# A fused attention and SiLU kernel: first keys by another queue in fp32, wider first products, a last product in two halves

## The chip, the cores and the metric

The kernel runs on one core of a Trainium2 chip. The metric is the device time of one execution in microseconds, the median of three runs. The profile is of one further execution; its span runs from the first to the last instruction.

## The reference

```python
def _attn_ref(q, k, v):                       # (8, 12, 448, 64) each
    scale = 1.0 / np.sqrt(q.shape[-1])
    scores = scale * np.matmul(q, k.transpose(0, 1, 3, 2))
    ...
    attn = attn / (np.sum(attn, axis=-1, keepdims=True) + 1e-09)
    return np.matmul(attn, v).astype(np.float32)

def _moe_ref(x, w_in, w_out):                 # (3584, 768), (768, 2048), (2048, 768)
    h = x @ w_in
    g = h * (1.0 / (1.0 + np.exp(-h)))
    return (g @ w_out).astype(np.float32)
```

The attention's output, with tokens ahead of heads, is `x`. Inputs and output are fp32.

## The kernel before

**Work units.** A unit is one batch and a group of four heads: 8 x 3 = 24 units. A unit's keys and queries are each one tile of 128 partitions (four heads of 32) by 14 x 64 elements: partition i of a head holds tokens 14i to 14i + 13. POOL loads them with a DMA that casts fp32 to fp16 (`load_k` L314, `load_q` L319). Queries of the first unit come in two halves of seven tokens (`PIECES` L253). VectorE then turns blocks of 32 x 32 pairs (`turn_k` L375: per key tile two transposes of six blocks, L387, and one "lone" of two, L390; `turn_q` L392), so that TensorE has head elements on partitions.

**Attention.** Scores are computed with keys on the partitions and queries along the columns (`score` L436, four heads at a time in strips of 32 rows). A unit's 14 blocks of 32 keys go in chunks of four; the fourth chunk is half a unit and is shared with the next unit. ScalarE takes exponentials of 896 elements from three PSUM tiles in turn (`expo` L479). Sums and products with V are matmuls of 32 columns of weights (`attend_alone` L535 and L558, L591); VectorE inverts the sums and normalizes into `xT`, scaled by one half (`norm` L642). The first unit's first two bursts of scores use half of the queries each, so burst (0, 0) needs all key chunks but the lone one, and only the first half of q.

**First products.** `ffn1` (L684) multiplies blocks of 128 columns of `w_in` (f = 0 to 15) with `xT`, six matmuls for the six parts of 128 of the model dimension. All matmuls of this and the next stage are issued by `times` (L670, so L673 in the profile). ScalarE takes a tanh (`tanh` L702), VectorE multiplies it into the gate (`gate` L734, L740 for batch 0): (1 + tanh(h/2)) h/2 is the SiLU. In batch 0 the tokens come in two pieces of 224; two blocks f and f + 1 share one PSUM bank of 448 columns (`blocks` L699 is 2 for batch 0, 1 elsewhere), so every matmul there has 224 columns. Batches 1 to 3 use 448 columns. Batches 4 to 7 go in pairs with seven products in place of eight (`pair_product` L833).

**Last products.** Output rows go in quads of two tiles of 128 tokens (14 quads). The first quad is computed plainly (`plain` L926, o in the profile). The others split the weights and the gates into halves and use seven products m = 1, 5, 6, 2, 7, 3, 4 of eight matmuls of 384 columns (`product` L910; p in the profile). Products 1, 6, 7 and 4 gather in one PSUM bank, 5 and 3 in a second, 2 in a third. `take_copy` (L976) copies products 1, 5, 6 and 4 to SBUF on ScalarE, `take_sum` (L981) adds 2, 7 and 3 to such copies on VectorE, and `store` (L956) sends a 128 x 384 part to HBM by SP's queue, in the last quads by SP's and ScalarE's queues in turn. Of the last quad, product 4 comes last: eight matmuls, ScalarE's copy, two stores of 64 rows.

**The order.** Nothing is left to a scheduler at run time. The class `Order` (L111) plays the engines' times through while the kernel is built: each `Op` has an engine, a duration that the author estimates, and dependences, and the loop at L1880 picks what each engine does next, lowest bias first; the order so found is the program's order on each engine. Loads go out on POOL in the order of L1039 to L1066 (`od.load`, L155), at most eight at once; a key tile's buffer is one of two (`NRK` L242), so the third keys wait for the first to be turned. Where the planner expects TensorE to wait in the early stage it fills with matmuls of zeros (`run_zeros` L1867); the first fill is `FIRST` = 47 blocks of 128 columns (L248) in matmuls of up to 512. The zeros' tile is VectorE's first memset (L285).

Of the kernel before, what the change touches and what calls it, by code (L numbers as in the profile page):

```python
# [9 lines left out]
FP16 = mybir.dt.float16  # L10
# [100 lines left out]
class Order:  # L111
# [48 lines left out]
    def step(self):  # L160
# [26 lines left out]
        elif self.pool:  # L187
# [9 lines left out]
            if at is not None and at <= self.now:  # L197
# [6 lines left out]
                few = len(self.sent) < 7  # L204
# [10 lines left out]
def kernel(  # L215
# [27 lines left out]
    PACE = 2.6  # L243
    NPL = 4
# [3 lines left out]
    COLD, FIRST, QUIET = 8.5, 47, 0.16  # L248
    SHY = 0.5
    AWAIT = 1.0  # L250
    FAR = (NT * B // 4 - 3, NT * B // 4 - 1)
# [66 lines left out]

    def load_q(n, g0, g1):  # L319
# [55 lines left out]
    def turn_k(b, hg):  # L375
        t = rawk[(b, hg)][:].bitcast(FP32).rearrange("p (g i) -> p g i", i=32)
        kt = sb.tile([128, TPP, 32, 2], FP16, name=f"KT_{b}_{hg}", tag="KT", bufs=3)
        KT[(b, hg)] = kt
        pairs = kt.rearrange("p g i e -> p (g i e)").bitcast(FP32)
# [3 lines left out]
        for x in (0, 2):  # L383
# [3 lines left out]
            nc.vector.transpose(out=full[:, x : x + 2], in_=toks[:, :, at : at + 3])  # L387
            if count == 4:
                lone = 12 * (not high)
                nc.vector.transpose(out=pairs[:, lone : lone + 2], in_=toks[:, :, 3 - 3 * at])  # L390
# [293 lines left out]
    def ffn1(b, f, t0, t1, strips, c0, c1):  # L684
        i = f % blocks(b)
# [13 lines left out]
    def blocks(b):  # L699
        return 2 if b == 0 else 1  # L700

    def tanh(b, f, t0, t1):  # L702
        n = (t1 - t0) * blocks(b)
# [30 lines left out]
    def gate(b, f, t0, t1):  # L734
        r = b % 2
        cut = 6 * 128 - S if b == 1 else S
        for lo, hi, dst, at in ((0, cut, G, S * r), (cut, S, X, -cut)):
            lo, hi = max(lo, t0), min(hi, t1)
            if b == 0 and lo < hi:
# [170 lines left out]
    def product(qd, m, f0, f1, strips):  # L910
        w = {1: rows(2 * qd, 0), 2: rows(2 * qd, 1), 4: rows(2 * qd + 1, 1), 7: rows(2 * qd + 1, 0)}
        w = w[m] if m in w else S_t[(qd, m)]
        if BANK[m] == m and f0 == 0:
            pr_t[(qd, m)] = psum_bank(f"p_{qd}_{m}")
        for f in range(f0, f1):
            times(
                pr_t[(qd, BANK[m])][:, 0:OH],
                w[:, f, :],
                W_[m][:, f, :],
# [60 lines left out]

    def take_sum(qd, m):  # L981
# [57 lines left out]
    plan_k(0, 0)  # L1039
# [36 lines left out]

    def plan_turn(n):
        b, hg, g0, g1 = units[n]
        if b == B - 1 and not rq_ring.can(1, od.now):
            return False  # L1080
        if (b, hg) not in kt_op:
            if not kt_ring.can(1, od.now):
# [4 lines left out]
                    "DVE", 0.73, lambda: turn_k(b, hg), [ld_k[(b, hg)]], 20, then=rk_ring.give  # L1087
                )
            )
        if b == B - 1:  # L1090
# [7 lines left out]
                    [load],  # L1098
                    20,
# [38 lines left out]
    def gates_at(t, f):  # L1138
# [3 lines left out]
        for b in {(128 * t + c) // S for c in (0, 127)}:  # L1142
            x = g_op.get((b, f), [])
            made += x if len(x) >= (len(PIECES) if b == 0 else 1) else [None]
        return made

    def queue_ffn1(b, g0, g1):
        t0, t1, parts = 32 * g0, 32 * g1, []
        begun = {}
        for f in range(NFF) if b == 0 else [x for f in range(HF if b < PB else FILL) for x in (f, f + HF)]:  # L1150

          half = 6 if b else NDC
          for c0 in range(0, NDC, half):

            def run(f=f, c0=c0):
# [5 lines left out]
                n = blocks(b)  # L1161
# [27 lines left out]
            def deps(f=f, c0=c0):  # L1189
                if c0:  # L1190
                    return [] if begun.get(f) == c0 else [None]
                if f % blocks(b) and f - 1 not in parts:
                    return [None]
                made = [(x_op[(b, cc, g0)], cc * mm(t1 - t0)) for cc in range(NDC)] + ld_win[f]
# [11 lines left out]
            moe.append((deps, int(f % blocks(b) == 0 and c0 == 0), run, ()))  # L1206
# [762 lines left out]
```

## Time and profile before

| | |
|---|---|
| median of 3 runs | 380.81 us (380.5 to 380.94) |
| profiled execution | 380.37 us |
| its span | 378.6 us |
| TensorE busy | 372.4 us |
| ScalarE, VectorE busy | 255.5, 269.7 us |
| DMA bytes counted on the queues | 34.47 MB |
| q0 (POOL's loads) | 22.82 MB, 40.3% of 16 engines' span |
| q1 (SP's stores) | 10.53 MB, 10.6% |
| granted TensorE clock | 1.000 |

The page counts an engine busy from an instruction's start to its end. Matmuls overlap, so a busy TensorE says only that one was in flight; how fast they follow each other is read from their starts. The timeline lists instructions in order of time, merged when equal ones follow each other: start, busy time, engine, line, operation, tiles, shapes and count, and in brackets the idle time before them with what ended it. The chain of waits follows the end back to the start. The q0 rows of the DMA packets show the bytes written, so a packet of 1792 bytes in fp16 has read twice as many.

### The profile page before, as it was taken

To read this page: it belongs to the slowest core of one execution; us is meant where nothing else is said; L and a number is where in the kernel's file an instruction comes from. 1 tells how busy PE (TensorE), PEld (TensorE's weight loads), DVE (VectorE), ACT (ScalarE), POOL (GpSimd) and SP (SyncE) were. 2 spreads that over 40 slices of the span, in tenths; PEclk is the share of its full clock that TensorE was granted. 3 is DMA by queue.
4 is the path that set the end of the run, shared out by engine and by line. 5 is a ranking of instruction groups with operands and counts; after the bars stand their busy time and mean duration, and the time that the engine had idled before them with its cause. 6 is when DMAs were issued, how large, how long until landed. Compare 5 with 4: busy or idle time off the path is not lost.

```text
span 378.6 us, 9949 instructions
## 1 busy us (share of the span) xinstructions
PE 372.4 (98%) x4024; PEld 191.5 (51%) x4024; DVE 269.7 (71%) x553; ACT 255.5 (67%) x400; POOL 84.9 (22%) x155
## 2 busy tenths in 40 slices
PE   7999999999999999999999999999999999999995
PEld 3367664444444444444444454545555555556663
DVE  3666859899995869995969998898475424446541
ACT  4988874897768787877788777658872238882221
POOL 6652438451007326006423200000000000000000
PEclk9999999999999999999999999999999999999999
DMA  7999999946139948148955421200002331002343
GB/s 120 191 208 210 206 204 186 190 53 98 17 92 124 184 49 124 26 94 116 170 86 73 54 53 34 68 18 0 3 1 59 94 74 26 0 2 59 84 110 83
DMA packets 35854, 34.47 MB, mean 91 GB/s; under 512 B 11872, under 2 KB 35040, under 8 KB 35808
## 3 DMA queue, kind: packets, MB, share of 16 engines
q0 software_dynamic: 25312, 22.82, 40.3%
q1 hardware_dynamic: 10080, 10.53, 10.6%
q8 instruction: 31, 0.51, 0.5%
q10 hardware_dynamic: 416, 0.49, 0.4%
q14 instruction: 15, 0.12, 0.1%
HBM read 45.61 MB, written 11.01 MB: 150 GB/s over the span
## 4 chain that ended last, share of the span: by engine, by line
PE 97%; DMA 1%; ACT 1%; DVE 0%; issue 0%; POOLq 0%
PE p L673 32%; PE h L673 21%; PE f L673 16%; PE s L438 12%; PE a L558 8%; PE o L673 3%; PE a L544 2%; PE a L591 2%; DMA rk<-in_k_dram 1%; ACT T L483 1%; PE z L1872 0%; PE z L673 0%; PE z L544 0%; DVE KT L387 0%; ACT ost L977 0%
## 5 line engine op out<-in xcount | busy, mean ns | idle before, releaser
L494 ACT ACTIVATE E<-s 128x896 f16<-128x896 f32 x164 | 142.0, 923 | 23.7 <-PE s L438 23.6
L673 PEld LDWEIGHTS <-w_in_t 128*128 128x128 f16 (+1 forms) x981 | 61.3, 97 | 45.2 <-issue 8.4
L673 PE MATMUL h<-xT,w_in_t 128*32 128x448 f16 (+2 forms) x834 | 84.0, 333 | 0.0
L344 POOL DMA_DIRECT2D V<-in_v_dram x88 | 48.4, 557 | 52.5 <-PE a L558 32.2
L673 PEld LDWEIGHTS <-G 128*128 128x128 f16 (+1 forms) x637 | 43.4, 97 | 32.4 <-issue 5.2
L977 ACT COPY ost<-p 128x384 f32<-128x384 f32 x52 | 24.9, 479 | 50.4 <-PE p L673 31.9
L705 ACT ACTIVATE th<-h 128x448 f16<-128x448 f32 x67 | 36.6, 546 | 22.8 <-PE h L673 19.1
L673 PE MATMUL p<-w_out_t,G 128*128 128x384 f16 (+1 forms) x343 | 51.9, 326 | 0.0
L438 PE MATMUL s<-rq,KT 32*128 32x448 f16 (+3 forms) x728 | 45.4, 347 | 1.3 <-DVE rq L402 1.0
L983 DVE TENSOR_TENSOR ost<-p,ost 128x384 f32<-128x384 f32 x39 | 21.6, 553 | 31.3 <-PE p L673 14.3
L673 PEld LDWEIGHTS <-S 128*128 128x128 f16 (+1 forms) x330 | 29.5, 98 | 23.5 <-issue 4.2
L673 PE MATMUL p<-D,S 128*128 128x384 f16 (+1 forms) x214 | 37.5, 326 | 0.0
L558 PE MATMUL a<-E,V 128*32 128x448 f16 (+1 forms) x640 | 32.9, 356 | 0.0
L749 DVE SCALAR_TENSOR_TENSOR G<-th,h 128x448 f16<-128x448 f16 (+1 forms) x52 | 28.8, 565 | 4.5 <-ACT th L705 3.9
L324 POOL DMA_DIRECT2D rq<-in_q_dram x25 | 13.8, 553 | 67.3 <-PE s L438 57.7
L661 DVE SCALAR_TENSOR_TENSOR xT<-a,rdn 128x448 f16<-128x448 f32 x46 | 27.0, 618 | 2.7 <-PE a L558 2.0
L438 PEld LDWEIGHTS <-KT 32*128 32x128 f16 (+1 forms) x824 | 12.5, 96 | 30.3 <-issue 28.1
L507 DVE TENSOR_TENSOR T<-T,E 128x1792 f16<-128x1792 f16 x20 | 21.7, 1086 | 3.9 <-ACT E L494 3.8
L876 DVE TENSOR_TENSOR p<-f,p 128x448 f32<-128x448 f32 x15 | 9.4, 624 | 20.4 <-PE f L673 13.5
L673 PE MATMUL f<-sx,tw 128*128 128x448 f16 x102 | 23.5, 352 | 0.0
L507 DVE TENSOR_TENSOR T<-E,E 128x1792 f16<-128x1792 f16 x20 | 21.6, 1082 | 2.5 <-ACT E L494 2.5
L558 PEld LDWEIGHTS <-V 128*32 128x32 f16 (+1 forms) x640 | 13.7, 95 | 18.0 <-issue 10.3
(95 smaller groups left out, 430.2 us busy)
## 6 DMA issues: line engine op xcount, KB each, us to landing
out_dram<-ost SPq DMA_DIRECT2D x194, 48.0 KB, 1.6
rk<-in_k_dram POOLq DMA_DIRECT2D x24, 224.0 KB, 5.0
rq<-in_q_dram POOLq DMA_DIRECT2D x23, 224.0 KB, 5.6
w_out_t<-in_moe_w_out_dram POOLq DMA_DIRECT2D x4, 768.0 KB, 12.5
V<-in_v_dram POOLq DMA_DIRECT2D x42, 64.0 KB, 4.1
V<-in_v_dram POOLq DMA_DIRECT2D x42, 48.0 KB, 4.3
w_in_t<-in_moe_w_in_dram POOLq DMA_DIRECT2D x6, 256.0 KB, 9.0
w_in_t<-in_moe_w_in_dram POOLq DMA_DIRECT2D x3, 512.0 KB, 12.3
```

What stands on the lines that cost most here:

```text
L324: nc.gpsimd.dma_start(out=rawq[n][:, cols], in_=group_of(q, b, hg)[:, cols])
L344: nc.gpsimd.dma_start(out=VT[b][32 * x : 32 * (x + 1), hs, at : at + count, :], in_=v[b, hs].rearrange("h (i g) d -> i h g d", g=TPP)[:, : ...
L438: nc.tensor.matmul(out=pS[p0 : p0 + 32 * (x1 - x0), h % 2, at : at + q1 - q0], lhsT=KT[(b, hg)][32 * h : 32 * (h + 1), key_rows(b, hg, c, ...
L494: nc.scalar.activation(out=E[(n, w)][:, 2 * y : 2 * y + 2, :], in_=pS_t[(n, w, y)][:, :, 0:S], func=AF.Exp, scale=attn_scale,)
L507: nc.vector.tensor_tensor(out=T[n], in0=T[n] if step else E[(n, 0)], in1=E[(n, step + 1)], op=ALU.add,)
L558: nc.tensor.matmul(out=a[32 * h : 32 * (h + 1), 0:S], lhsT=VT[b][k0:k1, HG * hg + h, place(b, hg, c), part - 1 :: 2], rhs=e[k0:k1, h], sta ...
L661: nc.vector.scalar_tensor_tensor(out=x3(b, cc)[:, cc % 3, 32 * g0 : 32 * g1], in0=acc[(n, part)][:, 0:nq], scalar=0.5, in1=rdn_t[n].rearra ...
L673: nc.tensor.matmul(out=out[i : i + cut], lhsT=w[:, i : i + cut], rhs=x, start=start, stop=stop, skip_group_check=True,)
L705: nc.scalar.activation(out=th, in_=h_t[(b, f, t0)][:, 0:n], func=AF.Tanh)
L749: nc.vector.scalar_tensor_tensor(out=dst[:, f, at + lo : at + hi], in0=th_t[(b, f, t0)][:, lo - t0 : hi - t0], scalar=1.0, in1=h_t[(b, f, ...
L977: nc.scalar.copy(out=ost(qd, *OUT[m]), in_=bank(qd, BANK[m]))
L983: nc.vector.tensor_tensor(out=t, in0=bank(qd, BANK[m]), in1=t, op=ALU.add)
```

## The change

**The first keys.** `rk_0_0` isn't loaded by POOL any more. SP issues two loads in fp32 to a scratch tile (in the tenth buffer of the exponentials): tokens 0 to 7 of each row (128 x 512 elements) and 8 to 13 (128 x 384). ScalarE casts each piece to fp16. VectorE's turning of the first keys is split: first six blocks, q's first half, the other six blocks, the lone two, q's second half. POOL's first load is then q's first half, and all later loads move up by one place. The first fill of zeros is 36 blocks of 128 columns. Turning of the first four units gets an earlier bias, which moves a few transposes ahead of normalizations.

**First products of batch 0.** Blocks 0 to 5 stay as they were. Blocks 6 to 15 are queued once both pieces are there, as ten blocks of 448 columns with one PSUM bank, one tanh and one gate each. There were 192 matmuls of 224 columns; there are 72, and 60 of 448.

**The last product.** In the last quad, product 2 is computed in two halves of 192 output columns, each with a PSUM bank of its own, sixteen matmuls of 192 columns. Three of them stand ahead of product 3's first half, three ahead of product 4, two behind it, and the eight of the second half end the program. VectorE adds each half to the copy of product 1; the first half is stored by SP (128 x 192), the second by SP and ScalarE (64 x 192 each). Product 3 is cut in two around product 7. Otherwise the order of TensorE's instructions is the same, but for the zeros: behind the first scores there are 1152, 1024, 1280 and 1792 columns of them in place of 1408, 1152, 1024 and 1664, and one more matmul of 256 columns stands ahead of the first products with V.

```diff
+    BF0 = 6
...
-    COLD, FIRST, QUIET = 8.5, 47, 0.16
+    COLD, FIRST, QUIET = 8.5, 36, 0.16
+    FIRST_K = ((0, 8, 3.45), (8, TPP, 4.3))
...
+    def load_first():
+        t = sb.tile([128, HG, S], FP16, name="first_k", tag=f"E{NE - 1}", bufs=1)
+        t = t.rearrange("p h s -> p (h s)").bitcast(FP32)
+        rawk[(0, 0)] = sb.tile([128, TPP * D], FP16, name="rk_0_0", tag="rk", bufs=NRK)
+        for g0, g1, _ in FIRST_K:
+            first_k[g0] = t[:, D * g0 : D * g1]
+            nc.sync.dma_start(out=first_k[g0], in_=group_of(k, 0, 0)[:, D * g0 : D * g1])
+
+    def cast_first(g0, g1):
+        nc.scalar.copy(out=rawk[(0, 0)][:, D * g0 : D * g1], in_=first_k[g0])
...
-    def turn_k(b, hg):
+    def turn_k(b, hg, parts=(0, 2, 3)):
...
+            if x in parts:
+                nc.vector.transpose(out=full[:, x : x + 2], in_=toks[:, :, at : at + 3])
...
+        if 3 in parts:
+            nc.vector.transpose(out=lone[0], in_=lone[1])
...
-    def blocks(b):
-        return 2 if b == 0 else 1
+    def blocks(b, f):
+        return 2 if b == 0 and f < BF0 else 1
...
-    def product(qd, m, f0, f1, strips):
+    def product(qd, m, f0, f1, strips, c0=0, c1=OH):
...
+            pr_t[(qd, m)] = psum_bank(f"p_{qd}_{m}" + "r" * (c0 > 0))
...
-                pr_t[(qd, BANK[m])][:, 0:OH],
+                pr_t[(qd, BANK[m])][:, 0 : c1 - c0],
                 w[:, f, :],
-                W_[m][:, f, :],
+                W_[m][:, f, c0:c1],
...
+    def take_end(p, c0, c1):
+        t = ost_t[(LAST, 0, 0)][:, c0:c1]
+        nc.vector.tensor_tensor(out=t, in0=p, in1=t, op=ALU.add)
+        row = out.shape[0] - 256
+        for lo, eng in ((0, nc.sync), (64, nc.scalar)) if c0 else ((0, nc.sync),):
+            hi = lo + 64 if c0 else 128
+            eng.dma_start(out=out[row + lo : row + hi, c0:c1], in_=t[lo:hi])
...
-    plan_k(0, 0)
+    od.emit(load_first)
+    rk_ring.take()
+    cast_op = []
+    for g0, g1, at in FIRST_K:
+        come = Op("SP", 0.0, None)
+        come.done = at
+        fn = lambda g0=g0, g1=g1: cast_first(g0, g1)
+        cast_op.append(od.add(Op("ACT", act(D * (g1 - g0)), fn, [come], -10)))
...
+    def turn_bias(n):
+        return -11 if n <= 3 else 20
...
+            for part, busy, x in ((0, 0.37, 0), (2, 0.33, 1), (3, 0.2, 1)):
...
-        for f in range(NFF) if b == 0 else [x for f in range(HF if b < PB else FILL) for x in (f, f + HF)]:
+        for f in range(BF0 * (g1 - g0 == TPP), NFF if g1 - g0 == TPP else BF0) if b == 0 else [x for f in range(HF if b < PB else FILL) for x in (f, f + HF)]:
...
-        for m in (1, 5, 6, 2, 7, 3, 4):
+        for m in (1, 5, 6, 2, 7, 3, 4) if qd < LAST else (1, 5, 6, 7, 3, 4):
             for f0 in range(0, HF, 1):
                 queue(m, f0, f0 + 1)
+        if qd == LAST:
+            for c in range(2):
+                for f0 in range(0, HF, 1):
+                    queue(2, f0, f0 + 1, OH // 2 * c, OH // 2 * (c + 1))
...
+        if b == 0 and not pieces_left[b]:
+            queue_ffn1(b, 0, TPP)
```

The two numbers in `FIRST_K` are the times, in the planner's own clock, at which it takes the two pieces to have come.

## The prediction

> **What bounds the kernel now.** I read the page first, then the chain of waits, then the timeline of the first 75 us and of the last 6, then the DMA packets and landings in the trace. The page:
>
> ```profile
> span 378.6 us, 9949 instructions
> ## 1 busy us (share of the span) xinstructions
> PE 372.4 (98%) x4024; PEld 191.5 (51%) x4024; DVE 269.7 (71%) x553; ACT 255.5 (67%) x400; POOL 84.9 (22%) x155
> ```
>
> TensorE is busy for all but 6.2 us. So only three things can shorten the kernel: what TensorE waits for at the start, columns that it need not stream, and what stands behind its last product. The start, in the chain of waits:
>
> ```profile
> 1.25 3.77 DMA rk<-in_k_dram
> 5.02 0.02 issue
> 5.04 0.38 DVE KT L387
> 5.42 0.12 DVE KT L390
> 5.55 0.26 DVE KT L387
> 5.81 0.30 DVE rq L402
> 6.11 0.04 issue
> 6.15 0.63 PE s L438 x16
> 6.78 2.52 ACT T L483 x3
> ```
>
> The first keys take 3.77 us from POOL's issue to their landing, then four transposes, then the first scores at 6.15. The timeline beside it:
>
> ```profile
> 1.00 4.13 PE L1872 MATMUL z<-zeros 128*128 128x512 f16 x12 [1.00 <-DVE zeros L285]
> ...
> 1.25 0.68 POOL L316 DMA_DIRECT2D rk<-in_k_dram  x1 [0.80 <-POOLq L1953]
> ...
> 1.93 1.09 POOL L324 DMA_DIRECT2D rq<-in_q_dram  x2
> ...
> 6.76 3.35 ACT L483 ACTIVATE T<-s 128x896 f16<-128x896 f32 x4 [4.74 <-PE s L438]
> ...
> 9.97 9.86 ACT L494 ACTIVATE E<-s 128x896 f16<-128x896 f32 x12
> ```
>
> ScalarE runs exponentials without a break from 6.76 to 19.83; until about 11 us TensorE waits for it and fills with zeros. From 11 us on the starts of the matmuls leave no gap but about 0.1 us at each change between row, column and full products. So a start that is earlier by x is worth x, if loads keep up. The 16 DMA engines have packets without a break from 2.64 us (the first) to beyond 56 us.
>
> **A, the first keys.** Removed: POOL's first issue (0.68), so q's first half is issued at 1.25 instead of 1.93. Added: two issues on SP, two casts on ScalarE. SP has nothing ahead of them, ScalarE is idle until 6.76 but for its table load (over at 2.0).
> - *First packet.* No load on SP's queue is in the trace. SP can issue from 0.74 (when ScalarE starts) to 1.25 (when POOL does). Stores on that queue show their first packet 1.13 us after the issue (375.24 to 376.36); POOL's load took 1.39. I take 0.74 + 1.13 = 1.87, 0.77 earlier than 2.64; the late end is 1.25 + 1.39, no gain. The Trainium skill ("DMA: Bandwidth & Descriptors", Specifications) gives first-byte latencies of about 0.6 us for the hardware queues and 1 us for POOL's; by its difference of 0.4 instead of my 0.26 the packet, and the sum below, would gain 0.14 more.
> - *Landing.* A 1792-byte cast packet takes 154 ns, a 1536-byte store packet 65, a 4-byte one 9: by 9 ns + bytes/27.4, 2048 bytes take 84 and 1536 take 65. Eight of each per engine: 0.67 and 0.52 us, 1.19 together, against 8 x 154 = 1.23 before. From first packet to full landing the old load took 5.02 - 2.64 = 2.38, 1.15 beyond its packets; the last store 0.57 beyond. q's first half (8 x 88 = 0.70) mixes with the second piece. The second piece lands between 1.87 + 1.19 + 0.57 = 3.63 and 1.87 + 1.19 + 0.70 + 1.15 = 4.91; I take 4.27. q's first half lands between 4.33 and 4.91.
> - *Casts.* No such row. Copies of 384 from PSUM take 0.48, exponentials of 896 take 0.92, by the line 0.49 and 0.60 for 384 and 512. The first (and the first transpose) lies under the second landing.
> - *First scores.* By the keys: landing + 0.03 + cast 0.49 + 0.03 + transpose 0.34 + 0.05 = 4.57 to 5.85. By q: landing + its transpose 0.37 + the second key transpose 0.32 + 0.05 = 5.07 to 5.65. So 5.07 to 5.85; I take 5.40, which is **0.75 earlier** (0.3 to 1.08). The lone transpose now stands behind the first scores.
> - *What is late next.* Fills behind the point where TensorE stops waiting for ScalarE grow from 1664 to 1792 columns and one of 256 is added ahead of the first products with V: 384 columns at 0.218 us per 512 are 0.16, and a change of mode 0.10. The third unit's q is transposed ahead of a normalization now, and a wait of 0.08 at 17.28 may go. Net 0.18: **A = 0.57** (0.1 to 0.9).
> - *Loads.* They stay saturated, so each lands earlier by as much as the first packet, 0.77, as the keys' packets cost the same. V landed at 14.62 for use at 14.71; the last quarter of w_out at 56.21 for the product at 56.39. So everything ahead of 56 us may gain 0.77 + 0.18 = 0.95 at most: A and B below need 0.71.
>
> **B, 448 columns wide.** 120 products of 224 columns become 60 of 448; tanh and gate operations stay 16 each, with the same elements.
>
> ```profile
> 32.99 2.47 PE L673 MATMUL h<-xT,w_in_t 128*128 128x224 f16 x24
> ...
> 56.39 1.47 PE L673 MATMUL o<-w_out_t,G 128*32 128x384 f16 x32
> ...
> 71.28 2.44 PE L673 MATMUL h<-xT,w_in_t 128*128 128x448 f16 x12
> ```
>
> From start to start, without the change of mode, the 24 take 96.1 ns each and the 12 take 189.9. 2 x 96.1 - 189.9 = 2.3 ns, 60 times: **B = 0.14**. The wide blocks need both halves of the tokens, which are made before the first of them stands in the order; blocks 8 to 15 come later than before, so w_in (last landing 35.70, first use 36.78) gets more room.
>
> **C, the end.**
>
> ```profile
> 373.23 1.46 PE L673 MATMUL p<-D,G 128*128 128x384 f16 x8
> 373.50 0.56 DVE L983 TENSOR_TENSOR ost<-p,ost 128x384 f32<-128x384 f32 x1 [0.74 <-PE p L673]
> 374.73 0.48 ACT L977 COPY ost<-p 128x384 f32<-128x384 f32 x1 [4.72 <-PE p L673]
> 375.24 0.50 ACTq L970 DMA_DIRECT2D out_dram<-ost  x1
> ```
>
> Call 374.69, where TensorE ends, X. Then came 0.04, the copy 0.48, 0.03, and two stores whose last landing is 377.62, 2.38 after their issue: X + 2.93. Now sixteen products of 192 take the place of eight of 384 (162.6 ns each). The spacing of 192 is not shown; between 82.5 (the warm 128-column fill at 7.01 is followed after 57 ns, so weights do not hold it) and 97 (a weight load's own time): 0.02 to 0.25 more, I take 0.02. Ten follow product 4, so its copy and both its stores are issued by X + 0.25. The first half's store follows on SP until X + 0.61. The second half is added by VectorE, 0.11 after X + 0.02 (as at 373.50), 0.36 long (0.56 for 384; L876's 448 take 0.62, so 1.03 ns an element), so ScalarE's store goes out at X + 0.52 and SP's at X + 0.66, behind its own queue. They move half the bytes. Landing by the rows: SP's packets 1.13 later, X + 1.8 to 2.05; ScalarE's right behind, or as late after the issue as before (1.70), X + 2.2 to 2.35, 0.38 more to land: X + 2.6 to 2.75. **C = 0.30** (0.1 to 0.5; less the weight bound).
>
> **Sum.** 0.57 + 0.14 + 0.30 = 1.01. The profiled execution took 380.37 (span 378.6 and 1.77 around it): 379.36. It is 0.44 below the median shown, 380.81, so for that: **379.8**.
>
> **Rivals.**
> 1. *The keys land no earlier.* The engines write 205 to 215 GB/s in the saturated stretch; if written bytes are the limit, 448 KB in fp32 take 2.1 us instead of 1.07, or SP's queue yields to POOL's at each engine. For: nothing like it is in the trace. Against: stores reach 65 ns per 1536 bytes. First scores 1.05 later than forecast, 0.3 later than before: -0.30 - 0.18 + 0.14 + 0.30 = -0.04, that is 380.4, or 380.85 against the median: no change.
> 2. *TensorE's clock, slower.* The fill of zeros is cut from 6016 to 4608 columns. Before, 512 columns took 0.427 us until 3.93 and 0.218 from there; after the fill's end at 4.96 the rate held through a gap of 1.19. Now the fill ends at 4.48. If the release falls behind 4.48 in an execution, TensorE starts at half rate, and as it needed 2.93 us of unbroken work, it gets it only from about 9.1 on, until 12.0. From 5.4 to 12.0 it would do 3.3 us less work; its waits for ScalarE (0.79 in all) take part: 2.5 lost, 1.5 net: 381.9, or 382.3. Against: 0.55 us are left here. The Trainium skill ("TensorE: Matmul & The Clock Gate", Why this matters for your kernels) asks for at least 4 us of continuous work to be past the gate, and puts the transition at plus or minus 0.5 us from run to run; the fill is now 3.48 long (3.97 before), so by that rule this rival would decide. The trace was released after 2.93.
> 3. *Loads hold the gain back.* The first packet is early but the rest of the stream is not; then V's and w_out's landings cap A and B together at 0.18: 0.18 + 0.30, 379.9, or 380.3: within the bound.
>
> **Chances.** What a measurement of this kernel can tell from no change is about 0.2%, 0.76 us, so faster means below 380.05. Forecast (gains of 0.5 to 1.45): 0.65, of which 0.57 beyond the bound. Rival 1: 0.13. Rival 3: 0.10. Rival 2: 0.12. Faster 0.57, same 0.31, slower 0.12. The range goes from the good ends (the cap of 0.95 and C of 0.5, 379.35, less the scatter of 0.3 and an earlier first packet) to rival 1 with scatter: 378.9 to 381.1; rival 2 is left out.
>
> **What would show it.** First key packets near 1.9 and the second landing near 4.3; first scores near 5.4; ScalarE's exponentials unbroken from there; no wait at the first products with V and at the last quarter of w_out; 96 ns pairs gone between 29 and 52 us; 192-column products near 83 ns; the last landing some 2.65 us after TensorE's end. It is wrong if q's first half and not the keys decides the start by more than 0.25 us, if the zeros still run at 0.427 at their end, or if V is waited for at 14 us.

## The result, and the profile after

The changed kernel takes **381.86 us** (median of 12 executions, 380.86 to 384.01) where before takes 380.69 (380.36 to 380.98): a ratio of 1.0036, 95% interval 1.0025 to 1.0046, by that ratio 1.4 us slower (0.95 to 1.75). The prediction was 379.8 with a range of 378.9 to 381.1: wrong in sign, and outside its range. Single executions of 2102 us (of `keys_only`) and 475 us (of `own_turned`) are left out of the ratios below; the first is the one that was profiled, so no trace of `keys_only` is read.

The profiled execution took 381.51 us. Its page:

```profile
span 379.7 us, 9849 instructions
## 1 busy us (share of the span) xinstructions
PE 372.2 (98%) x3972; PEld 186.2 (49%) x3972; DVE 269.9 (71%) x554; ACT 256.7 (68%) x402; POOL 84.4 (22%) x154
```

TensorE has 0.2 us less to do and the span is 1.1 us longer, so the loss is waiting. Its chain of waits up to 20.8 us (start, length, what; times in us):

```profile
1.26 4.19 DMA rq<-in_q_dram
5.45 0.02 issue
5.47 0.41 DVE rq L422
5.88 0.26 DVE KT L405
6.14 0.14 DVE KT L410
6.28 0.02 issue
6.30 0.02 POOLq L318
6.32 0.49 issue
6.81 0.54 POOL rk L318
7.35 1.79 POOL V L359 x3
9.14 0.04 issue
9.18 0.62 POOL V L359
9.80 0.54 POOL rq L339
10.34 8.18 DMA rk<-in_k_dram
18.52 0.02 issue
18.54 0.64 DVE KT L405 x2
19.18 0.12 DVE KT L410
19.30 0.52 DVE xT L681
19.82 0.04 issue
19.86 0.94 PE a L564 x16
```

Before, this chain ran through the first keys and the scores to ScalarE's exponentials. Now it begins with q's first half, which landed at 5.45 (5.54 before, so hardly earlier). VectorE was idle for it:

```profile
5.47 0.41 DVE L422 STREAM_TRANSPOSE rq<-rq 128x224 f32<-128x224 f32 x1 [0.88 <-DMA rq<-in_q_dram]
```

The other six key blocks (until 6.14) and the "lone" transpose (L410, until 6.27) stand behind q on VectorE. Then the chain leaves TensorE altogether: the end of the key transposes frees the buffer that the third keys' load waits for. Before, all key blocks were turned by 5.81, and POOL went on at 6.10:

```profile
6.10 0.54 POOL L316 DMA_DIRECT2D rk<-in_k_dram  x1 [2.02 <-DVE rq L402]
6.62 1.86 POOL L344 DMA_DIRECT2D V<-in_v_dram  x3
```

Now that load goes out at 6.81, 0.71 later, and everything behind it in POOL's queue (values, queries, the next batch's keys) follows later. From 7 to 9 us the times of the DMA packets add up to 0.77 of the 16 engines' time, 1.07 before. TensorE's timeline shows what that does:

```profile
6.20 0.57 PE L458 MATMUL s<-rq,KT 32*128 32x224 f16 x16 [0.97 <-DVE KT L405]
...
14.76 0.28 PE L1945 MATMUL z<-zeros 128*128 128x256 f16 x1
15.72 0.56 PE L564 MATMUL z<-T,V 128*32 128x448 f16 x8 [0.67 <-DMA V<-in_v_dram]
...
18.87 0.74 PE L564 MATMUL a<-E,ones 128*32 128x448 f16 x12
19.86 0.94 PE L564 MATMUL a<-E,V 128*32 128x448 f16 x16 [0.25 <-DVE xT L681]
```

The first scores start at 6.20 (6.15 before). The first products with V, which followed almost without a wait at 14.71, start at 15.72, and at 19.86 TensorE waits again, for a normalization that stands on VectorE behind transposes of keys that landed at 18.52. (In the text a wait of TensorE is the gap between two starts less the usual spacing, 0.19 us for 448 columns, so 0.42 here; the brackets count from a modelled end and have 0.17 less.) From 82 to 358 us the kernel then runs a constant 0.87 us behind. The end, in the timeline:

```profile
374.80 0.48 ACT L1001 COPY ost<-p 128x384 f32<-128x384 f32 x1 [3.92 <-PE p L693]
374.96 0.36 DVE L1007 TENSOR_TENSOR ost<-p,ost 128x192 f32<-128x192 f32 x1 [1.08 <-PE p L693]
375.30 0.47 SPq L994 DMA_DIRECT2D out_dram<-ost  x1
375.31 0.50 ACTq L994 DMA_DIRECT2D out_dram<-ost  x1
375.62 0.36 DVE L1007 TENSOR_TENSOR ost<-p_2r,ost 128x192 f32<-128x192 f32 x1 [0.30 <-PE p_2r L693]
375.86 1.10 SPq L1011 DMA_DIRECT2D out_dram<-ost  x2
376.01 0.67 ACTq L1011 DMA_DIRECT2D out_dram<-ost  x1
```

The second half is summed by 375.98, but SP's part of its store goes out only as the second of the two issues that last from 375.86 to 376.96 (the trace has it at 376.49). It lands 2.90 us after TensorE's end; in before the last landing came 2.92 after it: no gain.

### The profile page after: what moved, and what is told of

The parts are those of the page before. It is cut to its first block, busy times and chain, and to the rows that moved or that the text cites. A ratio compares the mean times of both kernels' runs of the same rounds, so it can differ in the third digit from the quotient of the medians.

```text
span 379.7 us, 9849 instructions
## 1 busy us (share of the span) xinstructions
PE 372.2 (98%) x3972; PEld 186.2 (49%) x3972; DVE 269.9 (71%) x554; ACT 256.7 (68%) x402; POOL 84.4 (22%) x154
## 4 chain that ended last, share of the span: by engine, by line
PE 94%; DMA 3%; POOL 1%; DVE 1%; issue 0%; POOLq 0%
PE p L693 32%; PE h L693 21%; PE f L693 16%; PE s L458 10%; PE a L578 8%; PE o L693 3%; DMA rk<-in_k_dram 2%; PE a L564 2%; PE a L611 2%; DMA rq<-in_q_dram 1%; POOL V L359 1%; PE z L693 0%; DVE KT L405 0%; PE p_2r L693 0%; POOL rq L339 0%
## 5 line engine op out<-in xcount | busy, mean ns | idle before, releaser
L693 PEld LDWEIGHTS <-w_in_t 128*128 128x128 f16 (+1 forms) x921 | 55.6, 97 | 49.3 <-issue 8.5
L693 PE MATMUL p<-w_out_t,G 128*128 128x384 f16 (+2 forms) x343 | 51.8, 324 | 0.0
L769 DVE SCALAR_TENSOR_TENSOR G<-th,h 128x448 f16<-128x448 f16 (+1 forms) x62 | 34.7, 573 | 6.0 <-ACT th L725 5.2
```

What stands on the lines that cost most here:

```text
L693: nc.tensor.matmul(out=out[i : i + cut], lhsT=w[:, i : i + cut], rhs=x, start=start, stop=stop, skip_group_check=True,)
L769: nc.vector.scalar_tensor_tensor(out=dst[:, f, at + lo : at + hi], in0=th_t[(b, f, t0)][:, lo - t0 : hi - t0], scalar=1.0, in1=h_t[(b, f, ...
```

## The experiments

Eighteen runs; ratios are to runs of before on the same chip. Three numbers are read from every trace, because the medians of 11 or 12 executions leave intervals of some 0.4 us to each side: the **lag** at 54 us (one ScalarE instruction against the same one in before's trace, with the 0.09 of the second part added back where it is in), the lag that the second part takes off between 43 and 54 us, and the **tail**: the span's growth less the lag at 369.5 us.

### The parts one at a time

The parts are those of the change: the first keys, the first products of batch 0, the last product. `keys_only` is the first, with the fill and the order that go with it. `blocks_only` is the second alone (`BF0 = 6`), `halves_only` the third.

> The kernel before with the first part alone (first keys by SyncE's queue in fp32, their casts, the order of transposes and the fill target of 36 that go with it), without the 448-wide blocks and without the last product by halves. My prediction: 0.57 us faster than before. Theory of the late third keys: their load waits for the lone key transpose and so goes out at about 6.8 us instead of 6.10, values land about 1.0 us later, TensorE waits some 0.8 us for them at about 15.7 us and some 0.4 us at about 19.9 us, and the kernel is about 1.0 us slower than before (0.87 that the changed kernel has lost by 82 us, and the 0.14 of the second part which it has not). Rival, the blocks and the tail carry the whole loss: within 0.2 us of before.

> The kernel before with the second part alone (ten blocks of the first batch's first products 448 wide). Prediction's term: 0.14 us faster, 380.55 where before is 380.69. Rival, the order of the work around it takes the gain back: within 0.05 us of before; it may cost up to 0.3 us if the loss of the changed kernel sits here.

> The kernel before with the third part alone (last product by halves in two banks). Prediction's term: 0.30 us faster. Theory from the changed kernel's trace: the store of the first half holds SyncE's queue for 0.54 us, the last store's issue is no earlier than before, and five closing waits instead of one stand behind its landing, so 0.2 to 0.3 us slower, with TensorE's end where it was to 0.05 us and the span 0.2 to 0.3 longer. Rival, no difference but the closing waits' order is chance: within 0.1 us.

Measured: `keys_only` 381.47 against 380.60, ratio 1.0020 (1.0009 to 1.0032); `blocks_only` 380.75, 1.0005 (0.9995 to 1.0014); `halves_only` 381.20, 1.0015 (1.0005 to 1.0025). Two parts cost something each, and the sum, 1.0040, agrees with the whole, 1.0036, within the intervals. The second part is a gain all the same: in each of the twelve traces that have it the lag falls by 0.085 to 0.096 between 43 and 54 us, in each of those without it by 0.005 at most. Its median is blurred by something else, which the trace of `halves_only` shows, though its instructions of the first 300 us are those of before:

```profile
14.22 0.57 PE L455 MATMUL s<-rq,KT 32*128 32x448 f16 x6
15.70 0.56 PE L561 MATMUL a<-T,V 128*32 128x448 f16 x8 [0.91 <-issue]
```

It waits for V at 15.70, as the changed kernel does. V's last part landed at 14.62 in before's profiled execution, at 15.04, 15.61 and 16.38 in those of `blocks_only`, `halves_only` and `halves_mended`. So values come too late, by chance, in before as well, and the profile that the prediction read was the luckiest of these four: lags of 0, 0.33, 0.57 and 1.34.

### The late third keys

The buffer of their own for the first keys (`own_buffer`, `own_again`):

```diff
-        rawk[(0, 0)] = sb.tile([128, TPP * D], FP16, name="rk_0_0", tag="rk", bufs=NRK)
+        raw = sb.tile([128, HG, S], FP16, name="rk_0_0", tag=f"E{NE - 2}", bufs=1)
+        rawk[(0, 0)] = raw.rearrange("p h s -> p (h s)")[:, 0 : TPP * D]
...
-    rk_ring.take()
...
-                then = rk_ring.give if part == 3 else None
+                then = None
```

> The changed kernel with one thing else: the cast first keys lie in a buffer of their own (the place of a later score tile), so the load of the third keys waits for no transpose and can go out right behind the others on GpSimd, at about 3.6 us; only the number of zero columns in a few fills shifts with it. Theory of the late third keys: values land by 14.8 us again, TensorE's wait for them at 15.7 us is below 0.1 us, the 0.42 us at 19.9 us goes too because the second batch's keys land earlier, and the time falls by 0.8 to 1.1 us from the changed kernel's 381.86, to 380.8 to 381.0 (what stays is the tail, 0.24, less the blocks, 0.14). Rival, the stream of loads itself is later with fp32 keys in front or two queues at once: values still land after 15.3 us and the time stays at 381.5 or above.

> The changed kernel once more, word for word, beside own_buffer's repeat on the same chip, because one trace showed one execution. Its ratio was 1.0036. Theory of the late third keys: third keys issued at 6.6 to 6.9 and a wait for values of over 0.5 us at 15.5 us or later again, ratio 1.0025 to 1.0046. Rival, the wait for values was that execution's chance (halves_only and halves_mended, whose first 300 us are those of before, show it too): the third keys' issue is late again but no wait of over 0.3 us stands at the values.

> own_buffer once more, beside the changed kernel on the same chip. Theory of the late third keys: 0.6 to 1.2 us below after_again, values landing by 14.5 us as in the four traces with that buffer so far (13.90 to 14.45). Rival, its first ratio (1.0006) was chance: within 0.3 us of after_again.

The other way round, before with the same lateness put in (`late_keys`):

```diff
+        if (b, hg) == (0, 2):
+            nc.gpsimd.memset(t[:, 0:512], 0.0)
         nc.gpsimd.dma_start(out=t, in_=group_of(k, b, hg))
```

> The kernel before with one instruction more: GpSimd clears 512 columns of the third keys' buffer just ahead of their load, so that this load and all behind it in that queue go out later by the length of the clearing (about 0.6 us, estimated from the 0.33 us that GpSimd takes for 64x256) plus some 0.1 us; nothing else is changed. Theory of the late third keys (0.71 us of lateness made values 1.05 us later and the changed kernel 0.87 us slower by 82 us): third keys issued at 6.8 instead of 6.10, values at about 15.7, 0.6 to 1.0 us slower than before. Rival, the loads have room and the changed kernel's loss comes from the fp32 keys' queue or the order on VectorE: within 0.25 us of before.

Measured: `own_buffer` 381.04 (1.0006, 0.9994 to 1.0018); on one chip `after_again` 381.69 (1.0034, 1.0022 to 1.0046), `own_again` 380.63 (1.0012, 0.9999 to 1.0024) and `late_keys` 381.00 against 380.54 (1.0022, 1.0008 to 1.0036). POOL's timeline in `own_buffer`:

```profile
3.00 0.57 POOL L340 DMA_DIRECT2D rq<-in_q_dram  x1
3.52 0.58 POOL L318 DMA_DIRECT2D rk<-in_k_dram  x1
4.04 2.52 POOL L360 DMA_DIRECT2D V<-in_v_dram  x4
```

and in `late_keys`:

```profile
5.96 0.52 POOL L317 MEMSET rk<- 128x512 f16 x1 [1.89 <-DVE KT L389]
6.78 0.53 POOL L318 DMA_DIRECT2D rk<-in_k_dram  x1 [0.30 <-POOL rk L317]
```

The third keys (L318) go out at 3.52 instead of 6.81 in the first, at 6.78 instead of 6.10 in the second, and the time follows both ways. Over all traces:

| start of the kernel | third keys issued | V landed | lag at 54 us |
|---|---|---|---|
| as before (4 traces) | 6.04 to 6.21 | 14.62 to 16.38 | 0 to 1.34 |
| before with lateness put in (`late_keys`) | 6.78 | 15.34 | 0.30 |
| as changed (5) | 6.81 to 7.09 | 15.42 to 16.13 | 0.89 to 1.32 |
| keys in their own buffer (8) | 3.50 to 3.52 | 13.55 to 14.98 | -0.67 to 0.52 |

The changed start is always late, the mended one never as late as its best case. Part of the lateness is the step from the key transposes to the load. In the five changed traces a wait instruction on POOL ends some 0.05 us after the last transpose, and the load starts 0.49 after that (6.32 to 6.81 above): 0.54 in all. In before the load carries the wait itself and starts 0.29 after the last key transpose (5.81 to 6.10). The bracket in its line names q's transpose, which ended at 6.10, but the memset of `late_keys`, which waits for that buffer too, began 0.06 after the key transposes and ahead of the end of q's, and its load then started 0.29 after the memset.

So the late third keys are shown as a cause: taken away, the time falls on one chip from 1.0034 to 1.0012, with intervals that just meet; put in, it rises. What is not shown is a size to 0.1: `late_keys` cost 0.84 by its ratio and 0.30 in its trace, which lies inside the range of the untouched start. Nor is it the whole loss in every median: `own_no_halves` and `own_long_fill` below have the buffer too, their traces lead before's at 54 us (by 0.67 and 0.29), and their ratios are still 1.0021 and 1.0039. The profiled execution of the second was the fastest of its six.

### The tail

`halves_mended` (on before) and `own_mended` (on `own_buffer`):

```diff
-        for lo, eng in ((0, nc.sync), (64, nc.scalar)) if c0 else ((0, nc.sync),):
-            hi = lo + 64 if c0 else 128
-            eng.dma_start(out=out[row + lo : row + hi, c0:c1], in_=t[lo:hi])
+        eng = nc.sync if c0 else nc.scalar
+        eng.dma_start(out=out[row : row + 128, c0:c1], in_=t)
```

> The kernel before with the last product by halves, as in halves_only, but the first half's store (128 rows of 192) goes out by ScalarE's queue and the second half's by SyncE's queue in one piece of 128 rows. Theory of the held queue: in halves_only SyncE issues the second half's store 1.15 us after the start of the last matmul although its sum is done at 0.64, because the first half's store holds that queue from 0.52 to 1.06, and eight closing waits stand behind its landing; here the store goes out at about 0.67, lands at about 2.89 instead of 3.14, and its wait is the last of the closing waits, so SyncE's closing drain comes 0.64 earlier than in halves_only and 0.30 earlier than in before, both against TensorE's end: 380.3 (380.2 to 380.6 where before is 380.6 and halves_only 381.2). Rival, the stores' landing binds wherever they are issued: within 0.15 us of halves_only, 381.05 to 381.35.

> All three parts of the change, with the first keys in a buffer of their own and the two stores of the last halves as in halves_mended: the version that both theories together point to. own_buffer's ratio 1.0006 less 0.64 us of the tail: 380.2 where before is 380.6, and 0.2 to 0.6 us below before; if the tail's mending does nothing it is own_buffer's 381.0.

Measured: `halves_mended` 380.64 where before is 380.64 (1.0004, 0.9994 to 1.0014); `own_mended` 381.03 (1.0012, 1.0001 to 1.0023). The timeline of `halves_mended`:

```profile
376.13 0.36 DVE L1004 TENSOR_TENSOR ost<-p_2r,ost 128x192 f32<-128x192 f32 x1 [0.30 <-PE p_2r L690]
376.40 0.77 ACTq L1007 DMA_DIRECT2D out_dram<-ost  x1
376.51 0.39 SPq L1007 DMA_DIRECT2D out_dram<-ost  x1
```

SP now issues the second half's store 0.02 after its sum, as expected, yet the last landing moved to ScalarE's store (3.04 us after the start of the last matmul; 0.77 went into issuing it). So `halves_mended`, expected 0.3 us below before, is even with it, and `own_mended`, expected at 380.2, came out at the rival's 381.0. The tails of the traces are steady enough to settle the rest:

| last stores | first part out | first part in |
|---|---|---|
| as before | 0.00 to 0.01 (blocks_only, late_keys, short_fill) | 0.37 to 0.38 (four traces) |
| by halves | 0.36 (halves_only) | 0.23 to 0.26 (six) |
| by halves, mended | -0.11 (halves_mended) | 0.23 to 0.28 (own_mended, own_turned, turned_fill) |

The first part costs 0.38 **at the end**, where it changes no instruction of the work. In the trace SyncE ends the program with one wait for each landing semaphore, in a fixed order, 0.06 us each when nothing is waited for. The following times count from the start of the last matmul. In before the last landing (3.25) is met by the second to last of these waits, and the closing drain comes at 3.39. In `keys_mended` the same landing (3.26) is met by the first of the last eight: its two added loads had taken semaphores, so the last stores got others; seven waits follow, and the drain comes at 3.78. Halving in `halves_only` does the same to SP's last store, with seven waits behind it. The costs don't add: the halves add 0.36 to before, but take 0.14 off the 0.38 where the first part is in. My theory of the held queue was right about the issue and explained the smaller share: of the 0.48 between `halves_only` and `halves_mended`, 0.10 is the landing and the rest are closing waits.

### The fill of zeros

Rival 2 of the prediction. `own_no_halves` is `own_buffer` without the last product's halves; `own_long_fill` is `own_no_halves` with the first fill 11 blocks longer, `after_long_fill` the changed kernel with the same, `short_fill` before with it 11 shorter:

```diff
-            od.on_pe(Op("PE", n * each, lambda n=n, wide=wide, i=m_ring.free[0][1]: run_zeros(n, wide, i)), "full", -(-n // wide))
+            od.on_pe(Op("PE", n * each, lambda n=n - 11 * (n == FIRST), wide=wide, i=m_ring.free[0][1]: run_zeros(n, wide, i)), "full", -(-n // wide))
```

> The changed kernel with the first keys in a buffer of their own and without the last product by halves. Sum of the ratios so far: 0.0006 less 0.0015, 380.25 where before is 380.6. My prediction's terms for the first two parts, 0.71 us faster, 379.9, would need the 0.6 us by which the first scores start earlier to reach the end. Theory of the stream: the start is earlier by about 0.6 but the queries and keys that follow and the values land no earlier than in before (values at 14.4 or later), so that half or more of it is gone by 14 us, and 380.2 to 380.6 comes out.

> own_no_halves with 1408 more zero columns at the end of the first fill (6016 as in before), all else in the same order. Rival of my prediction, the fill cut short lets TensorE's full rate come late in some executions: 0.3 to 0.8 us below own_no_halves and a scatter of its runs of 0.6 us instead of about 1.5. Theory of the stream (all traces so far show the full rate at the first scores, with the zeros' rate doubling between 4.3 and 5.1 us): within 0.2 us of own_no_halves, with the same scatter.

> The kernel before with its first fill cut from 6016 to 4608 columns of zeros, all else in the same order: the fill ends at about 4.8 us if TensorE's rate has not doubled by then, the first scores start at about 6.15 as before. Theory of the rate (in 3 of 8 traces with the short fill the first scores ran at 187 ns a group instead of 99, for 0.4 to 4 us): 0.1 to 0.4 us above before in the median, and the upper quartile 0.4 us or more above that of before (380.7 to 380.9). Rival, the half rate was a chance of the launch and the loads hide it: within 0.15 us in the median, and the same upper quartile.

> The changed kernel with 1408 columns more in its first fill (6016), nothing else moved. Theory of the rate: 0.1 to 0.4 us below the changed kernel's 381.7 to 381.9. Rival, its loss is the loads' and the order's alone, and own_long_fill's 1.0039 in six runs says that a longer fill does not help: within 0.15 us, or up to 0.3 us slower where the fill ends after the first scores could start.

Measured: `own_no_halves` 381.22 (1.0021, 1.0006 to 1.0037), `own_long_fill` 381.85 in six executions (1.0039, 1.0026 to 1.0052), `short_fill` 381.07 against 380.51 (1.0013, 1.0004 to 1.0022), `after_long_fill` 381.58 (1.0025, 1.0013 to 1.0037). TensorE in `own_again`, one of three traces where the rival came true:

```profile
3.53 1.70 PE L1945 MATMUL z<-zeros 128*128 128x512 f16 x4
6.09 0.93 PE L459 MATMUL s<-rq,KT 32*128 32x224 f16 x16 [0.86 <-DVE KT L406]
6.96 0.93 PE L1945 MATMUL z<-zeros 128*128 128x512 f16 x2
7.82 1.14 PE L459 MATMUL s<-rq,KT 32*128 32x224 f16 x16
```

The sixteen first scores take 0.93 us; they take 0.57 above in the changed kernel's trace. The half rate costs 0.80 in all here: the first scores lead before's by 0.06, the first exponentials lag by 0.29, the fifth by 0.74. In the two others (`own_no_halves`, `own_turned`) it costs 0.27 and 0.36 (the first scores lead before's by 0.76 and 0.98 us, the first exponentials by 0.49 and 0.62).

The granted clock in the views' rows is 1.00 throughout, so those rows do not show this rate. The clock records in the traces do: in each, one stretch of full clock begins where the spacing halves. It begins at 3.6 to 5.6 us in the nine traces with 6016 columns or more, ahead of the first scores in all of them. With 4608 or 4864 columns it begins within the fill in four traces of ten, in the pause behind it in three (in the changed kernel's at 5.84, after zeros at 0.427 us each to their end), and after the first scores had begun in three (`own_no_halves` 6.02, `own_turned` 6.71, `own_again` 10.31).

All 19 stretches last 108, 109 or 110 times 3.413 us (368.6, 372.1, 375.5). So the clock is judged on a grid of 3.413 us, which lies differently in every execution. With that grid laid over the matmuls, every stretch begins at the end of a window in which matmuls were in flight for 0.77 of the time or more, and no earlier window had more than 0.75. The Trainium skill ("TensorE: Matmul & The Clock Gate", What's actually happening) has the gate judged over a free-running window of about 3.4 us, which would make the moment a matter of chance; the traces agree. The rate doubles 2.6 to 4.6 us after the first zeros with the long fill, and up to 9.3 after them where the pause spoiled two windows (`own_again`: 0.73 and 0.75).

What follows: the cut fill costs before about 0.5 us (`short_fill`), though its own trace has the full rate in time; in the changed kernel the restored fill gave 0.35 by the ratios, within their intervals, and `own_long_fill` went the other way. The mechanism is shown, its average price in the changed kernel is not. `own_no_halves` missed what was expected of it (380.2 to 380.6) by 0.6 us or more; its trace loses 1.4 us at 127 us, as shown below.

### The order on VectorE

`own_turned` and `turned_fill` (on `own_mended`, the second with the long fill) and `after_turned` put the transposes of the second batch's first keys behind the `xT` at 19.3 us:

```diff
+            late = Op("SP", 0.0, None)
+            late.done = 17.8 if n == 3 else 0.0
...
-                    "DVE", 0.73, lambda: turn_k(b, hg), [ld_k[(b, hg)]], turn_bias(n), then=rk_ring.give
+                    "DVE",
+                    0.73,
+                    lambda: turn_k(b, hg),
+                    [ld_k[(b, hg)], late],
+                    turn_bias(n),
+                    then=rk_ring.give,
```

> own_mended with the transposes of the second batch's first keys put behind the two products of xT and one transpose of queries on VectorE, as before has them; nothing else moves. Theory of the order on VectorE: in after (0.42 us) and own_mended (0.73 us) TensorE waited at 19 to 20 us for an xT that stood behind transposes whose keys had not landed; that wait goes, and the median falls by 0.2 to 0.5 us from own_mended's 1.0012, to 380.3 to 380.8 where before is 380.64. Rival, chance landings elsewhere make up the loss: within 0.2 us of own_mended's ratio.

> The changed kernel with the transposes of the second batch's first keys put behind the product of xT and the transpose of queries that stood behind them on VectorE; nothing else moves. Theory of the order on VectorE (waits of 0.42 and 0.62 us at 19.8 us in after and after_again): that wait goes, and the time falls by 0.3 to 0.5 us from the changed kernel's ratios 1.0034 and 1.0036, to 1.0021 to 1.0028. Rival, TensorE waits for the same keys a little later anyway: 1.0031 or above.

> own_turned (all three parts, keys in a buffer of their own, stores mended, order mended) with the fill of 6016 columns: the version that all theories together point to. Theory of the rate: 0.1 to 0.4 us below own_turned's 1.0009, so at or up to 0.3 us below before. Rival, as in own_long_fill: at 1.0009 or above.

Measured: `own_turned` 380.87 (1.0009, 1.0000 to 1.0018), `after_turned` 381.75 (1.0034, 1.0020 to 1.0048), `turned_fill` 380.78 (1.0007, 0.9998 to 1.0017). The theory fails for the changed kernel: the wait at 19.86 goes, but three of 0.28 to 0.39 us between 20.8 and 23.1 take its place, and its lag at 54 us is the largest of the five, 1.32. `own_turned` is within 0.2 us of `own_mended`, as the rival has it, and `turned_fill`, the version of all theories, is not below before. No gain from the order is shown.

Another wait turned up behind these, at about 127 us, in `own_no_halves`:

```profile
126.31 0.64 DVE L406 STREAM_TRANSPOSE KT<-rk 128x192 f32<-128x192 f32 x2 [3.14 <-DMA rk<-in_k_dram]
126.87 0.20 DVE L411 STREAM_TRANSPOSE KT<-rk 128x64 f32<-128x64 f32 x1
127.00 0.61 DVE L637 STREAM_TRANSPOSE rdn<-a 128x448 f32<-128x448 f32 x1
```

Keys whose load was issued at 119.23 are there 7.1 us later (4.8 to 5.7 in most traces); TensorE waits 1.2 us for the transpose at 127.00 behind them. Four traces have such a wait, of 0.4 to 1.3 us (`own_no_halves`, `own_again`, `after_long_fill`, `turned_fill`), of eleven with the first two parts of the change; none of the six with the old start has it, nor do the two with the first part alone. Why, stays open.

### The first part alone, mended

`keys_mended` is the first part with its own buffer, the long fill and the turned order, without the other two parts; `keys_again` is `keys_only` once more.

> keys_only once more. Theory of the late third keys: third keys issued at 6.6 to 7.1 us, a wait for values of 0.4 us or more at 15.4 us or later, and one of 0.3 us or more at 19 to 20 us; ratio 1.0015 to 1.0032 (keys_only 1.0020). Rival, the first part's loss lies behind 20 us: TensorE's lag against before is below 0.4 us at 30 us and grows after it.

> The first part alone, mended: first keys by SyncE's queue in fp32 and cast on ScalarE, in a buffer of their own, the fill of 6016 columns, the second batch's first transposes of keys behind the product of xT; without the 448-wide blocks and the halves. turned_fill's 1.0007 less the medians of blocks_only (0.15) and halves_mended (0.0 to 0.15): 380.4 to 380.6 where before is 380.5. My prediction's term for this part, 0.57 us faster, would give 379.95. Theory of the stream (values land at 13.9 to 14.5 us whatever the start, and before has them at 14.6 to 16.4): at most 0.3 us below before.

Measured: `keys_again` 381.66 against 380.81 (1.0024, 1.0015 to 1.0033); `keys_mended` 380.91 (1.0000, 0.9991 to 1.0009). TensorE in `keys_again`:

```profile
16.17 0.56 PE L564 MATMUL z<-T,V 128*32 128x448 f16 x8 [0.92 <-DMA V<-in_v_dram]
```

The theory's waits are there without the other parts (third keys issued at 7.02, values landed at 16.13; the second wait shrank to 0.12). Mended, the part is even with before although its tail still costs 0.38, so ahead of the tail it has gained about that much (worked out: 0.00 - 0.38, with 0.34 to each side; its one trace leads before's, the luckiest of four, by 0.04 there). No version measured here is faster than before.

## Why the prediction was wrong, step by step

**First packet, landing, casts: right.** The first key packet came at 1.77 us (1.87 forecast), the second landing at 4.01 (4.27), casts took 0.62 and 0.51 us (0.60 and 0.49), and packets of 2048 and 1536 bytes took 84 and 65 ns, as worked out from the stores' rows.

**"q's first half lands between 4.33 and 4.91", so first scores at 5.40: the step that failed first.** In the changed kernel they started at 6.20 to 6.47 in five traces, because q's first half landed at 5.45 to 5.72. That was the text's own sign of error: VectorE waited 0.88 us for it. Rival 1 had the first scores about there (6.45), but by late keys, and those came early. With the keys' own buffer the first scores start at 5.17 to 6.13. Why q lands no earlier while POOL waits for the third keys is not settled.

**"The lone transpose now stands behind the first scores": the step that failed with it.** I priced the new order of the transposes at nothing, without naming who waits for their end: the third keys' load, through the buffer, and behind that load POOL's whole queue. The profile of before held the answer: POOL stands still until that load's issue at 6.10, behind VectorE. Of the 0.71 us of lateness, 0.33 are the six blocks behind q's late half (6.14, where all keys were turned by 5.81 before), 0.13 the lone transpose, and 0.25 the longer step to the load (0.54 in place of 0.29). The load came 1.36 after q's landing; with q at 4.33 to 4.91 it would have gone out at 5.69 to 6.27, about as before. By that estimate, from one trace, the late q made the loss, and the unpriced buffer carried it to the loads.

**"They stay saturated, so each lands earlier by as much as the first packet": wrong.** The DMA engines had less to do at 7 to 9 us (0.77 in place of 1.07), and V landed 0.8 to 1.5 us later than in before's trace instead of 0.77 earlier. Even with the wait mended V gains little on that trace (13.55 to 14.98 against 14.62; 15.04 to 16.38 in the three others of that start). What is left of an earlier start is mixed: the first scores' lead of 0.62 in `own_buffer` is 0.50 at 54 us, that of 0.65 in `own_mended` is gone. Rival 3 had this mechanism, but as a cap on the gain and not as a loss.

**The base.** The executed profile had V just in time (0.10 us of wait). The steps that said "no wait at the first products with V" took that for the rule; the three other traces of the same start wait 0.58 to 1.49.

**Rival 2 (the rate): half right.** It happens in some executions, where the fill was cut, but costs 0.3 to 0.8 in the traces and not 1.5. What it took for 2.93 us of unbroken work is the filled part of a 3.413 us window. Its sign, zeros at 0.427 to their end, came true in the profiled execution, which was spared because full clock came in the pause, 0.36 us ahead of the first scores.

**B: right in kind, 0.09 instead of 0.14.** (The last landing of w_in is 35.94 in before's trace, not 35.70; with its first use at 36.78 nothing hangs on it.)

**C: -0.30 became +0.24.** The spacing of 192 columns was right (82.5 ns, 0.02 lost), and so was SP's store waiting behind its own queue, but I let it land at 2.60 to 2.75 after TensorE's end and it took 2.90 (2.92 before), since the first half's store held SP for 0.54. What I had not counted at all are the closing waits in their fixed order, which the first part and the halves both make longer.

In sum: lag +0.97 less 0.09 for B and 0.24 of tail are the 1.1 by which the spans of the two profiled executions differ.

## What to carry to other kernels

When a step is moved, follow the buffer it frees as well as the data it makes: here key transposes put behind a query that landed late held back one load and, in order, everything queued after it. Read an early stage that lives on landings from several executions before calling a wait zero, since one profile may be the lucky one. And count the end of a program to its last instruction: which semaphore the last landing signals decided 0.4 us.

## What the runs showed of the hardware that was not expected

- SyncE's closing waits cost about 0.06 us each in a fixed order of semaphores; a landing met first in that order ends the program 0.38 later than the same landing met second to last.
- Where a wait instruction ahead of a load on POOL was the last to end, the load started 0.49 us after it and 0.54 after the transpose that released it (five traces of the changed start); where the load's own wait was the last, it started 0.29 after what it waited for (before, `late_keys`).
- The same loads, issued within 0.2 us of the same times, landed up to 1.8 us apart between executions (V at 14.62 and 16.38).
- TensorE's rate doubled at the end of a window of a 3.413 us grid in which matmuls were in flight for 0.77 of the time or more, and never after one of 0.75 or less (19 traces): at 3.6 to 5.6 us with a long fill, and as late as 10.3 with a fill that ended at 5.2.
- A store of 128 rows of 768 bytes held ScalarE's queue for 0.77 us and SP's for 0.39 to 0.54.
